# Token tiles of 1024 and 512 columns, one group's weights resident, x blocks streamed

## The chip, the cores and the metric

One of the eight cores of a Trainium2 chip runs the whole program in one launch. The metric is the device time in microseconds. An engine here is TensorE (PE), VectorE (DVE), ScalarE (ACT), GpSimd (POOL) or SyncE (SP, which issues nearly all DMAs).

## The reference, cut to what matters

A linear attention feeds two feed-forward layers. There are 8 x 576 = 4608 tokens, 512 model columns and 2048 hidden columns, all in float32.

```python
kv  = einsum('bhsd,bhse->bhde', k, v);  out = einsum('bhsd,bhde->bhse', q, kv)
x   = out / sqrt(mean(out*out, -1) + 1e-6) * g_norm        # to (4608, 512)
h   = x @ moe_w_in;   r = maximum(h, 0);  x = (r*r) @ moe_w_out       # relu layer
h   = x @ moe2_w_in;  out = (h * cos(h)) @ moe2_w_out                 # cos layer
```

The weights come in as float64 bit patterns and are turned into float32 on the chip.

## The kernel before, in words

Every float32 operand of a large product is split into a high and a low float32r part, and a product is three matmuls: high x high, high x low, low x high.

**First part.** Attention runs beside the first half of the relu layer's hidden columns, in 72 chunks (a tile of 512 tokens and one block of 128 hidden columns each). The layer's partial result goes to DRAM as `p_d`, the attention's output as `x_d`.

**Second part, in slots.** The rest of the relu layer and the whole cos layer run in a list of slots `(m, t, q)`: layer m (0 relu, 1 cos), token tile t, group q of 512 hidden columns. The relu layer has 2 groups left, the cos layer 4. Tiles are of 768 tokens, so there are 6: 12 relu slots (0 to 11) and 24 cos slots (12 to 35). The order is layer, tile, group: a tile goes through all its groups before the next tile starts.

A slot's *first product* (x times w_in) is a Winograd-Strassen scheme with 7 block products instead of 8: 7 phases of 12 matmuls in `ORDER`. It needs 7 x blocks `xb` (sums and differences of quarters of the tile, each split in two) and 7 weight tiles `wi`. `keep` (ACT), `add` (DVE) and `last` (ACT) empty the accumulators, a chain of `relu_*` or `cos_*` steps with `g_hi` (ACT) and `g_lo` (DVE) makes the operand g. The *second product* (g times w_out, 4 weight tiles `wo`) runs in units of 12 matmuls; `drain` adds each into a partial sum `part` that stays in SBUF for all groups of the tile.

Before, `prep_load` and `prep_block` make the next tile's x blocks and write them to `xb_d`; `load_xb` reads each block once per tile, and `load_wi` and `load_wo` read 11 tiles of 512 KB in every slot. `conv_w` of kind "pair" prepares the cos layer's w_in (`wi_d`) during the relu slots.

**What sets the order.** A list of jobs, each at a position in slots (`at(pos(...), fn)`), is sorted and run between matmuls; 84 first-product steps make one slot, and second-product steps of the slot before stand between them, `LAG2` later. The tile framework then places buffers and semaphores; every engine works its instructions in order, SP's DMAs too.

Of the kernel before, what the change touches and what calls it, by code (L numbers as in the profile page):

```python
# [22 lines left out]
def kernel(  # L23
# [31 lines left out]
    BIG = 768  # L55
    HT = BIG // 2
    NBIG = NT // BIG
# [20 lines left out]
    y_d = [dram.tile([P, NKC, BIG], F32, name=f"y_d{t}") for t in range(NBIG)]  # L78
    xb_d = {
        (m, t, i): dram.tile([P, 2, 2, HT], F32, name=f"xb_d{m}_{t}_{i}")  # L80
        for m in range(2)
        for t in range(NBIG)
# [73 lines left out]
    def conv_w(kind, m, f, i):  # L156
        raw = raws.pop((kind, m, f, i))
        if kind == "pair":
# [8 lines left out]
            h, l = (hl_p.tile([P, NPR, P], F32R, tag="hl", name="hl") for _ in "hl")  # L167
# [3 lines left out]
            for k, x in enumerate((h, l)):  # L171
                nc.sync.dma_start(out=wi_d[m, q][:, :, k, pp, i, :], in_=as32(x[:]))  # L172
# [170 lines left out]
    def units(b):  # L343
        return [(b, p, i) for p in range(NKC) for i in range(2)]
# [60 lines left out]
    BLOCKS = {(0, 0): 2 / 7, (1, 1): 5 / 7, (0, 1): 6 / 7, (1, 0): 1.0}  # L405
    xb, wi, wo, kept, hs, ys, parts = {}, {}, {}, {}, {}, {}, {}

    def prep_load(m, t, c, stay):
        if stay:
            raw = xb_p.tile([P, 2, BIG], F32, tag="xb", name="xraw")  # L410
        else:
            raw = pools["raw"].tile([P, 2, BIG], F32, tag="r", name="xraw")
        xraw[m, t, c] = raw
        if m == 0:
            for b, s, done, n in pieces(t * BIG, BIG, S):
                nc.sync.dma_start(out=raw[:, :, done:done + n], in_=x_d[b][:, c::2, s:s + n])
        else:
            nc.sync.dma_start(out=raw, in_=y_d[t][:, c::2, :])

    def prep_block(m, t, c, i, stay):  # L420
        raw = xraw[m, t, c]
        b11, b12, b21, b22 = (raw[:, a, s] for a in range(2) for s in (slice(0, HT), slice(HT, BIG)))
        if i in (0, 1, 4):
            src = {0: b11, 1: b21, 4: b22}[i]
        else:
            new = temp([P, HT], F32, f"xt{i}")
            x, y = {
                2: lambda: (b12, b11),
                3: lambda: (b22, xraw[m, t, c, 2][:]),
                5: lambda: (b22, b12),  # L430
                6: lambda: (b21, xraw[m, t, c, 3][:]),
            }[i]()
            nc.vector.tensor_tensor(out=new, in0=x, in1=y, op=ALU.subtract)
            xraw[m, t, c, i] = new
            src = new[:]
        if stay:
            if (m, t, i) not in xb:
                xb[m, t, i] = xb_p.tile([P, 2, 2, HT], F32R, tag="xb", name="xb")
            h, l = (xb[m, t, i][:, k, c, :] for k in range(2))
        else:  # L440
            both = temp([P, 2, HT], F32R, "xhl")
            h, l = both[:, 0, :], both[:, 1, :]
        nc.scalar.copy(out=h, in_=src)  # L443
        nc.vector.tensor_tensor(out=l, in0=src, in1=as32(h), op=ALU.subtract)
        if not stay:
            nc.sync.dma_start(out=xb_d[m, t, i][:, :, c, :], in_=as32(both[:]))

    def load_xb(m, t, i):
        xb[m, t, i] = x = xb_p.tile([P, 2, 2, HT], F32R, tag="xb", name="xb")
        nc.sync.dma_start(out=as32(x[:]), in_=xb_d[m, t, i][:])  # L450

    def load_wi(k, i):
        m, t, q = slots[k]
        wi[k, i] = w = w_p.tile([P, 2, 2, 2, P], F32R, tag="w", name="wi")
# [56 lines left out]
    def cos_1(k, b):  # L511
        ys[k, b] = y = temp([P, 2, HT], F32, "y")
        nc.scalar.activation(out=y[:].bitcast(I32), in_=hs[k, b], func=AF.Identity, bias=zerob)  # L513

    def cos_2(k, b):
        y = ys[k, b]
        nc.vector.scalar_tensor_tensor(  # L517
            out=y, in0=y[:].bitcast(I32), scalar=-1.0, in1=hs[k, b], op0=ALU.mult, op1=ALU.add
# [16 lines left out]
    def g_hi(k, b):  # L535
        gs[k, b] = g = pools["g"].tile([P, 2, 2, HT], F32R, tag="g", name="g")
        nc.scalar.copy(out=g[:, 0], in_=ys[k, b])  # L537

    def g_lo(k, b):
        g = gs[k, b]  # L540
        nc.vector.tensor_tensor(out=g[:, 1], in0=ys.pop((k, b)), in1=as32(g[:, 0]), op=ALU.subtract)  # L541

    def load_parts(t):
        for i in range(NKC):
            parts[0, t, i] = e = w_p.tile([P, BIG], F32, tag="w", name="part")
            for b, s, done, n in pieces(t * BIG, BIG, TOK):
                nc.sync.dma_start(out=e[:, done:done + n], in_=p_d[b][:, i, s:s + n])

    s_count = [0]
    units_of = (2 * NKC, BIG // P)  # L550

    def second_unit(k, n):
        m, t, q = slots[k]
        half = units_of[m] // 2
        j, i = 1 - n // half, n % half
        ps = bank_of(f"acc{s_count[0] % 4}")
        s_count[0] += 1
        if m == 0:
            ps = ps[:, :HT]
# [16 lines left out]
    def drain(k, j, i, ps):  # L576
        m, t, q = slots[k]
        final = q == groups_of[m][-1]
        if m == 0:
            e = parts[0, t, i][:, j * HT:(j + 1) * HT]  # L580
# [14 lines left out]
        if final:  # L595
            r0 = t * BIG + r * P
            nc.sync.dma_start(out=out[r0:r0 + P, :], in_=e)
# [5 lines left out]
    LAG2 = 1.2  # L603
# [8 lines left out]
    class Stream:  # L612
# [10 lines left out]
        def place(self, positions, after, skip=()):  # L623
            for k, (n, item) in enumerate(zip(positions, self.items)):
                at(n, self.use, *item)
                if k not in skip:
                    at(n + (after if n < nA0 else after / 12), self.advance)
# [26 lines left out]
    for b, (s0, ds) in enumerate(starts):  # L654
        for i, u in enumerate(units(b)):
# [17 lines left out]
    def prep(m, t, c, n0, n1, stay=False):  # L673
        at(n0 - (1.0 if stay else 0.1), prep_load, m, t, c, stay)
        for a, i in enumerate((0, 1, 2, 3, 5, 4, 6)):
            at(n0 + (n1 - n0) / NPR * a, prep_block, m, t, c, i, stay)

    for c in range(2):
        prep(0, 0, c, nAtt + 3 + 9 * c, nAtt + 11 + 9 * c, True)
    for k, (m, t, q) in enumerate(slots):  # L680
        if q:
            continue
        if k:
            for f, i in enumerate(ORDER):
                at(pos(k - 1 + f / 7 + 0.03), load_xb, m, t, i)
        following = (m, t + 1) if t + 1 < NBIG else (m + 1, 0)
        if following[0] < 2:
            n0, n1 = max(pos(k - 0.9), pos(0.2)), pos(k + len(groups_of[m]) - 1.05)
            half = (n1 - n0) / 2
            for c in range(2):  # L690
                prep(*following, c, n0 + c * half, n0 + (c + 0.9) * half)
    for k, (m, t, q) in enumerate(slots):
        early = 0.4
        for f, i in enumerate(ORDER):
            at(pos(k + f / 7 - early) if k else nA0 - 5 + f / 2, load_wi, k, i)
        for c in range(4):
            at(pos(k + LAG2 - early + 0.02 * c), load_wo, k, c)
        if m == 0 and q == 0:
            at(pos(k + LAG2 - 0.2), load_parts, t)
        at(pos(k + 1 / 7), keep, k, "m1", 0)  # L700
        at(pos(k + 2 / 7), add, k, (0, 0), 1, "m1")
        at(pos(k + 3 / 7), keep, k, "u2", 3)
        at(pos(k + 4 / 7), keep, k, "m5", 2)
        at(pos(k + 5 / 7), add, k, (1, 1), 5, "m5")
        at(pos(k + 6 / 7), add, k, (0, 1), 4, "u2")
        at(pos(k + 1.0), last, k)
        chain = (cos_1, cos_2, cos_3, cos_4, cos_5, g_hi, g_lo) if m else (relu_1, relu_2, g_hi, g_lo)
        for b, s0 in BLOCKS.items():
            for a, fn in enumerate(chain):
                at(pos(k + s0 + 0.04 * (a + 1)), fn, k, b)  # L710
# [128 lines left out]
```

## Time and profile before

| | |
|---|---|
| median of 3 runs | 1847.97 us (1846.03 to 1854.89) |
| the profiled execution | 1847.94 us, its span 1846.2 us |
| PE busy in the span | 1703.8 us, 92% |
| DVE, ACT busy | 1108.0 us (60%), 968.9 us (52%) |
| moved by DMA | 500.2 MB, mean 271 GB/s |
| granted TensorE clock, mean | 0.974 |

The span runs from the first instruction to the last. Busy shares are averages over parts with different limits, so the rows further down are cut by stretch. Matmuls overlap each other, and the records' durations of one matmul are longer than the distance between two. A line such as L475 is a line of the kernel; `FB<-xb,wi` is what an instruction writes and reads.

### The profile page before, as it was taken

To read this page: it belongs to the slowest core of one execution; us is meant where nothing else is said; L and a number is where in the kernel's file an instruction comes from. 1 tells how busy PE (TensorE), PEld (TensorE's weight loads), DVE (VectorE), ACT (ScalarE), POOL (GpSimd) and SP (SyncE) were. 2 spreads that over 40 slices of the span, in tenths; PEclk is the share of its full clock that TensorE was granted. 3 is DMA by queue.
4 is the path that set the end of the run, shared out by engine and by line. 5 is a ranking of instruction groups with operands and counts; after the bars stand their busy time and mean duration, and the time that the engine had idled before them with its cause. 6 is when DMAs were issued, how large, how long until landed. Compare 5 with 4: busy or idle time off the path is not lost.

```text
span 1846.2 us, 23727 instructions
## 1 busy us (share of the span) xinstructions
PE 1703.8 (92%) x8624; PEld 1456.2 (79%) x8624; DVE 1108.0 (60%) x1766; ACT 968.9 (52%) x1556; POOL 82.7 (4%) x74
## 2 busy tenths in 40 slices
PE   5899999999996978787878899999999999999998
PEld 3676777777785968777778798888888888888887
DVE  6866676767736555545453446666665656655554
ACT  4766677764425343433433446555565656555453
POOL 0102121221000000000000000000000000000000
PEclk9999999999998999898989999999999999999999
DMA  7655677654579999999999977987987888878551
GB/s 277 195 172 163 217 242 219 186 166 147 166 249 309 369 346 368 369 355 368 355 344 355 396 279 267 333 296 257 330 289 268 322 296 280 294 243 321 186 202 41
DMA packets 233093, 500.19 MB, mean 271 GB/s; under 512 B 19600, under 2 KB 133264, under 8 KB 232976
## 3 DMA queue, kind: packets, MB, share of 16 engines
q1 hardware_dynamic: 232208, 496.31, 77.7%
q0 software_dynamic: 768, 2.36, 0.3%
q8 instruction: 68, 1.11, 0.2%
q14 instruction: 49, 0.40, 0.1%
HBM read 365.69 MB, written 132.91 MB: 270 GB/s over the span
## 4 chain that ended last, share of the span: by engine, by line
PE 60%; DMA 10%; DVE 3%; SPq 2%; ACT 2%; issue 1%; DVEq 0%; ACTq 0%
PE SA L570 15%; PE SB L570 14%; PE FA L475 12%; PE FB L475 12%; DMA wo<-wo_d 2%; DMA wi<-wi_d 2%; PE FA L360 2%; PE SB L395 2%; PE SA L395 2%; PE FB L360 1%; DMA xraw<-x_d 1%; DMA xb_d<-xhl 1%; DMA xraw<-y_d 1%; DMA xb<-xb_d 1%; SPq L172 1%
## 5 line engine op out<-in xcount | busy, mean ns | idle before, releaser
L475 PE MATMUL FB<-xb,wi 128*128 128x384 f32 x1512 | 406.5, 347 | 40.7 <-ACT m L486 20.4
L475 PE MATMUL FA<-xb,wi 128*128 128x384 f32 x1512 | 402.9, 342 | 33.1 <-DMA wi<-wi_d 16.1
L475 PEld LDWEIGHTS FB<-xb,wi 128*128 128x128 f32 x1512 | 284.7, 194 | 54.8 <-ACT m L486 22.3
L475 PEld LDWEIGHTS FA<-xb,wi 128*128 128x128 f32 x1512 | 280.5, 191 | 45.4 <-issue 15.2
L570 PE MATMUL SB<-wo,g 128*128 128x512 f32 x864 | 309.7, 398 | 0.8 <-DVE part L590 0.8
L570 PE MATMUL SA<-wo,g 128*128 128x512 f32 x864 | 309.6, 398 | 0.8 <-DVE part L590 0.8
L570 PEld LDWEIGHTS SB<-wo,g 128*128 128x128 f32 x864 | 160.0, 187 | 37.8 <-DVE part L590 3.9
L570 PEld LDWEIGHTS SA<-wo,g 128*128 128x128 f32 x864 | 160.0, 187 | 37.5 <-DVE part L590 3.7
L513 ACT ACTIVATE y<-h,zerob 128x768 int32<-128x768 f32 x96 | 90.1, 939 | 167.0 <-DVE h L492 166.5
L570 PE MATMUL SA<-g,wo 128*128 128x384 f32 x576 | 143.8, 361 | 22.6 <-DMA wo<-wo_d 18.2
L570 PEld LDWEIGHTS SA<-g,wo 128*128 128x128 f32 x576 | 108.6, 203 | 33.7 <-DMA wo<-wo_d 24.6
L570 PE MATMUL SB<-g,wo 128*128 128x384 f32 x576 | 129.5, 343 | 5.2 <-DVE part L581 5.2
L531 DVE SCALAR_TENSOR_TENSOR y<-y,h 128x768 f32<-128x768 f32 x96 | 91.7, 955 | 63.6 <-ACT y L527 63.6
L443 ACT CAST xhl<-xraw 128x384 fp32r<-128x384 f32 x66 | 33.2, 505 | 175.6 <-DMA xraw<-x_d 120.9
L517 DVE SCALAR_TENSOR_TENSOR y<-y,h 128x768 f32<-128x768 int32 x96 | 91.7, 955 | 41.6 <-ACT y L513 40.1
L570 PEld LDWEIGHTS SB<-g,wo 128*128 128x128 f32 x576 | 105.4, 194 | 7.2 <-DVE part L581 7.0
L360 PE MATMUL FA<-xh,wh 128*128 128x512 f32 x240 | 99.3, 414 | 5.9 <-ACT xh L329 3.7
L541 DVE TENSOR_TENSOR g<-y,g 128x768 fp32r<-128x768 f32 x96 | 91.7, 956 | 21.6 <-ACT g L537 20.7
L537 ACT CAST g<-y 128x768 fp32r<-128x768 f32 x96 | 80.1, 834 | 46.5 <-DVE y L531 46.4
L523 ACT ACTIVATE y<-y 128x768 f32<-128x768 f32 x96 | 81.3, 847 | 43.1 <-DVE y L517 42.2
L360 PE MATMUL FA<-xl,wh 128*128 128x512 f32 x240 | 96.9, 404 | 0.1
L360 PE MATMUL FA<-xh,wl 128*128 128x512 f32 x240 | 96.1, 400 | 0.0
(154 smaller groups left out, 2676.4 us busy)
## 6 DMA issues: line engine op xcount, KB each, us to landing
wi<-wi_d SPq DMA_DIRECT2D x252, 512.0 KB, 5.9
wo<-wo_d SPq DMA_DIRECT2D x144, 512.0 KB, 6.5
xb_d<-xhl SPq DMA_DIRECT2D x154, 384.0 KB, 4.8
xb<-xb_d SPq DMA_DIRECT2D x77, 768.0 KB, 7.8
wi_d<-hl SPq DMA_DIRECT2D x48, 448.0 KB, 3.8
kvld<-in_kv SPq DMA_DIRECT2D x32, 512.0 KB, 6.9
raw<-in_wA SPq DMA_DIRECT2D x24, 512.0 KB, 4.1
q<-in_qT SPq DMA_DIRECT2D x32, 288.0 KB, 4.1
```

The source lines that it names most:

```text
L172: nc.sync.dma_start(out=wi_d[m, q][:, :, k, pp, i, :], in_=as32(x[:]))
L360: nc.tensor.matmul(ps, a[:, 0, cs], m[:], start=(c == 0 and k == 0), stop=(c == NKC - 1 and k == 2))
L395: nc.tensor.matmul(o, a[:, cs], m[:], start=(f == 0 and n == 0), stop=(f == NH - 1 and n == 2), skip_group_check=True)
L443: nc.scalar.copy(out=h, in_=src)
L475: nc.tensor.matmul(ps[:, pp, :], a, b, start=(i in (0, 1, 2) and n == 0), stop=(n == 5), skip_group_check=True)
L513: nc.scalar.activation(out=y[:].bitcast(I32), in_=hs[k, b], func=AF.Identity, bias=zerob)
L517: nc.vector.scalar_tensor_tensor(out=y, in0=y[:].bitcast(I32), scalar=-1.0, in1=hs[k, b], op0=ALU.mult, op1=ALU.add)
L523: nc.scalar.activation(out=y, in_=y, func=AF.Sin, scale=math.pi)
L531: nc.vector.scalar_tensor_tensor(out=y, in0=y, scalar=-2.0 * math.pi, in1=hs.pop((k, b)), op0=ALU.add, op1=ALU.mult)
L537: nc.scalar.copy(out=g[:, 0], in_=ys[k, b])
L541: nc.vector.tensor_tensor(out=g[:, 1], in0=ys.pop((k, b)), in1=as32(g[:, 0]), op=ALU.subtract)
L570: nc.tensor.matmul(ps, lhs, rhs, start=(n == 0), stop=(n == 11), skip_group_check=True)
```

## The change

- Token tiles are four of 1024 and one of 512 (`TILES`, with half size ht): matmuls of the first product have 512 or 256 columns instead of 384, and so have the relu layer's second ones.
- The list of slots is ordered layer, group, tile: 10 relu slots (0 to 9, of which 4 and 9 are the tile of 512) and 20 cos slots. A group's 11 weight tiles are loaded once, and stay for its five slots.
- In a layer's first pass (q = 0) `load_quads` reads a tile's quarters and `x_block` makes the blocks right before use, and writes them to `xb_d`; in later passes `x_block` reads both halves back, 1.9 sevenths of a slot ahead.
- Partial sums no longer stay in SBUF: `load_ev` brings each unit's sum in, `drain` adds, and the result is written to `y_d` or `o_d` (`out` in the last pass).
- A weight pair's low half is written into its raw tile, not into a tile of its own. Buffers: 13 tiles of 4 KB per partition for x, 16 for h, y and g; a pad of 96 bytes moves the tiles of the first part, and all operands of the large products then start at multiples of 128 bytes.

```diff
-    BIG = 768
-    HT = BIG // 2
-    NBIG = NT // BIG
+    BIG = 1024
+    TILES = [(t0, min(BIG, NT - t0) // 2) for t0 in range(0, NT, BIG)]
...
-            h, l = (hl_p.tile([P, NPR, P], F32R, tag="hl", name="hl") for _ in "hl")
+            p_h, tag = (pools["h"], "w") if pools["h"] is w_p else (pools["h"], "x")
+            h = p_h.tile([P, NPR, P], F32R, tag=tag, name="wh")
+            l = a.bitcast(F32R)[:, 1:]
...
-    slots = [(m, t, q) for m in range(2) for t in range(NBIG) for q in groups_of[m]]
+    slots = [(m, t, q) for m in range(2) for q in groups_of[m] for t in range(len(TILES))]
...
+    def x_block(k, i):
+        m, t, q = slots[k]
+        ht = TILES[t][1]
+        h, l = xb[k, i] = [big("x", F32R, f"x{n}", ht) for n in "hl"]
+        if q:
+            for a, x in enumerate((h, l)):
+                nc.sync.dma_start(out=as32(x), in_=xb_d[m, t, i][:, a])
+            return
...
+        if i == 3:
+            quads[m, t, "t1"] = combine(b12, b11)
+            quads[m, t, "t2"] = combine(b22, quads[m, t, "t1"])
...
         nc.scalar.copy(out=h, in_=src)
         nc.vector.tensor_tensor(out=l, in0=src, in1=as32(h), op=ALU.subtract)
+        for a, x in enumerate((h, l)):
+            nc.sync.dma_start(out=xb_d[m, t, i][:, a], in_=as32(x))
...
+    def load_ev(k, j, i):
+        m, t, q = slots[k]
+        t0, ht = TILES[t]
+        evs2[k, j, i] = e = temp([P, 512], F32, "ev")
+        if m:
+            r = j * (ht // P) + i
+            if q:
+                nc.sync.dma_start(out=e, in_=o_d[t].rearrange("p c n -> p (c n)")[:, r * DM:(r + 1) * DM])
+        elif q:
+            nc.sync.dma_start(out=e[:, :ht], in_=y_d[t][:, i, j * ht:(j + 1) * ht])
+        else:
+            for b, s0, done, n in pieces(t0 + j * ht, ht, TOK):
+                nc.sync.dma_start(out=e[:, done:done + n], in_=p_d[b][:, i, s0:s0 + n])
...
+        e = evs2.pop((k, j, i))
...
             nc.vector.tensor_tensor(out=e, in0=ps, in1=e, op=ALU.add)
-            if final and j == 0:
-                nc.sync.dma_start(out=y_d[t][:, i, :], in_=parts.pop((0, t, i)))
+            nc.sync.dma_start(out=y_d[t][:, i, j * ht:(j + 1) * ht], in_=e)
...
-    LAG2 = 1.2
+    LAG2 = 1.18
...
-        (pairs_in(1, range(2 * NP)), pos(0.4), pos(10)),
+        (pairs_in(1, range(2 * NP)), pos(2.5), pos(9.2)),
...
+    PH = 1 / 7
     for k, (m, t, q) in enumerate(slots):
+        if q == 0:
+            at(pos(k - 3.2 * PH) if k else nA0 - 6, load_quads, m, t)
         for f, i in enumerate(ORDER):
+            lead = 1.5 if q == 0 else 1.9
+            at(pos(k + (f - lead) * PH) if k or f > 2 else nA0 - 4 + f, x_block, k, i)
+            if t == 0:
+                at(pos(k + (f - 5.5) * PH) if k else nA0 - 5 + f / 2, load_wi, m, q, i)
+        if t == 0:
+            for c in range(4):
+                at(pos(k + LAG2 - 0.3 + 0.02 * c), load_wo, m, q, c)
...
+            at(pos(k + LAG2 + (n - 1.5) / len(todo)), load_ev, k, *u)
...
+        right("pad", 1).tile([P, 24], F32, name="pad")
...
+        pools["x"] = pools["h"] = ctx.enter_context(tc.tile_pool(name="xb", bufs=13, side="left"))
...
+    pools["c"] = ctx.enter_context(tc.tile_pool(name="c", bufs=16, side="left"))
+    pools["t"] = ctx.enter_context(tc.tile_pool(name="t", bufs=8, side="left"))
+    pools["h"] = w_p
```

SP's queue in the cos layer, before (L446 writes a made x block to DRAM, L450 reads one, L455 and L460 load weights):

```order
L446 DMA xb_d_2_6_159<-xhl 256x1x384
L460 DMA wo<-wo_d_11_206 128x1024
L455 DMA wi<-wi_d_3_186 128x1024 x4
L446 DMA xb_d_3_0_160<-xhl 256x1x384
L450 DMA xb<-xb_d_2_1_154 128x1536
L455 DMA wi<-wi_d_3_186 128x1024
L450 DMA xb<-xb_d_2_3_156 128x1536
```

The same queue in a later pass of the cos layer, after (L432 reads the halves of an x block, L563 a partial sum, L614 writes one):

```order
L614 DMA o_d_96<-ev 128x512
L563 DMA ev<-o_d_96 128x512
L432 DMA xh<-xb_d_2_0_150 128x1024
L432 DMA xl<-xb_d_2_0_150 128x1024
L563 DMA ev<-o_d_96 128x512
L614 DMA o_d_96<-ev 128x512
L563 DMA ev<-o_d_96 128x512
L432 DMA xh<-xb_d_2_1_151 128x1024
L432 DMA xl<-xb_d_2_1_151 128x1024
```

The weight loads are gone from between the x loads, and writes of drained units, which wait for DVE, now stand there.

DVE in the relu layer's first pass, before, while a weight pair is prepared (L433 and L444 make x blocks, L129 to L169 the pair, L541 a low part of g, L581 a drain):

```order
L129 TENSOR_SCALAR e<-raw 128x512
L131 TENSOR_SCALAR w<-raw 128x512
L444 TENSOR_TENSOR xhl<-xt_6516,xhl 128x384
L134 SCALAR_TENSOR_TENSOR w<-raw,w 128x512
L541 TENSOR_TENSOR g<-h,g 128x768
L137 SCALAR_TENSOR_TENSOR e<-raw,e 128x512
L433 TENSOR_TENSOR xt_6572<-xraw,xt_6516 128x384
L162 SCALAR_TENSOR_TENSOR raw<-w,e 128x512
L581 TENSOR_TENSOR part<-SA,part 128x384
```

The same in slot 2 after (L438 and L454 make x blocks, L129 to L171 the pair, L504 a sum, L549 a low part of g, L601 a drain):

```order
L454 TENSOR_TENSOR xl<-xraw,xh 128x1024
L549 TENSOR_TENSOR gl<-h,gh 128x1024
L601 TENSOR_TENSOR ev<-SA,ev 128x512
L601 TENSOR_TENSOR ev<-SB,ev 128x512
L129 TENSOR_SCALAR e<-raw 128x512
L131 TENSOR_SCALAR w<-raw 128x512
L134 SCALAR_TENSOR_TENSOR w<-raw,w 128x512
L137 SCALAR_TENSOR_TENSOR e<-raw,e 128x512
L601 TENSOR_TENSOR ev<-SB,ev 128x512
L162 SCALAR_TENSOR_TENSOR raw<-w,e 128x512
L504 TENSOR_TENSOR h<-FA,m_6150 128x1024
```

DVE's x work moved from halves of the next tile, long ahead, to whole blocks of the slot that is about to start, and its instructions are 1024 wide.

## Rows read from the trace of the kernel before

**Rows 1.** Busy time in four windows of the second part; columns first.
```profile
core 0: us, PE busy (x) PEld busy (x) DVE busy (x) ACT busy (x) POOL busy (x), PEclk, DMA share, GB/s
548.70:1049.10 500.40, 402.97 (x2071) 380.60 (x2070) 260.06 (x471) 204.66 (x301) 0.00 (x0) 0.92 0.99 357
1049.10:1084.60 35.50, 31.49 (x164) 30.30 (x163) 16.06 (x23) 15.83 (x21) 0.00 (x0) 0.90 0.75 288
1084.60:1787.90 703.30, 703.22 (x3439) 621.26 (x3438) 426.74 (x543) 397.81 (x521) 0.00 (x0) 1.00 0.80 281
1787.90:1846.20 58.30, 52.24 (x243) 43.81 (x241) 27.68 (x34) 22.04 (x27) 0.00 (x0) 1.00 0.25 90
```

**Rows 2.** Timeline of PE: first matmul of slots 0, 12, 13 (start, us).
```profile
548.74 0.34 PE L475 MATMUL FA<-xb,wi 128*128 128x384 f32 x1
...
1049.13 1.55 PE L475 MATMUL FA<-xb,wi 128*128 128x384 f32 x8
...
1084.57 0.33 PE L475 MATMUL FB<-xb,wi 128*128 128x384 f32 x1
```

**Rows 3.** DMA, 548.7 to 1049.1 us: total; issues, KB, us to landing.
```profile
DMA packets 99177, 178.45 MB, mean 357 GB/s; under 512 B 6351, under 2 KB 70607, under 8 KB 99148
wi<-wi_d SPq DMA_DIRECT2D x77, 512.0 KB, 8.4
xb<-xb_d SPq DMA_DIRECT2D x41, 768.0 KB, 9.5
wo<-wo_d SPq DMA_DIRECT2D x44, 512.0 KB, 9.0
```

**Rows 4.** Waits in that stretch: us in total, times, longest.
```profile
ACT xhl L443 <- DMA xraw<-x_d: 120.9, 9, 19.1
PE SA L570 <- DMA wo<-wo_d: 17.3, 10, 5.4
PE FB L475 <- DMA wi<-wi_d: 16.7, 8, 6.3
```

**Rows 5.** Chain that ended last, three places: start, us, matmuls.
```profile
482.88 2.80 PE FA L360 x12
...
1149.80 1.57 PE FB L475 x9
1151.37 1.85 PE SB L570 x8
...
1824.11 2.72 PE SB L570 x12
```

**Rows 6.** DMA between 1084.6 and 1787.9 us, as rows 3.
```profile
DMA packets 64732, 197.57 MB, mean 281 GB/s; under 512 B 6171, under 2 KB 22299, under 8 KB 64689
xb<-xb_d SPq DMA_DIRECT2D x35, 768.0 KB, 6.6
```

**Rows 7.** DVE instructions by line: busy, mean ns | idle before.
```profile
L541 DVE TENSOR_TENSOR g<-y,g 128x768 fp32r<-128x768 f32 x96 | 91.7, 956 | 21.6 <-ACT g L537 20.7
L444 DVE TENSOR_TENSOR xhl<-xt,xhl 128x384 fp32r<-128x384 f32 x88 | 48.7, 554 | 23.8 <-ACT xhl L443 22.4
L590 DVE TENSOR_TENSOR part<-SB,part 128x512 f32<-128x512 f32 x60 | 41.2, 686 | 33.3 <-PE SB L570 32.8
```

**Rows 8.** The same view: DVE work on one weight pair.
```profile
L134 DVE SCALAR_TENSOR_TENSOR w<-raw,w 128x512 uint32<-128x512 uint32 x64 | 44.0, 688 | 1.1
L131 DVE TENSOR_SCALAR w<-raw 128x512 uint32<-128x512 uint32 x64 | 26.8, 419 | 0.0
L166 DVE TENSOR_TENSOR raw<-raw 128x128 f32<-128x128 f32 x96 | 26.5, 317 | 0.6
L169 DVE TENSOR_TENSOR hl<-raw,hl 128x896 fp32r<-128x896 f32 x24 | 26.2, 1090 | 6.6 <-ACT hl L168 6.1
```

**Rows 9.** DMA issues of the whole run.
```profile
raw<-in_wA SPq DMA_DIRECT2D x24, 512.0 KB, 4.1
p_d<-ev SPq DMA_DIRECT2D x18, 512.0 KB, 4.6
```

More of the change, by code (lines that the diff above doesn't have):

```diff
@@ L77 @@
     p_d = [dram.tile([P, NKC, TOK], F32, name=f"p_d{t}") for t in range(NTILE)]
-    y_d = [dram.tile([P, NKC, BIG], F32, name=f"y_d{t}") for t in range(NBIG)]
+    y_d = [dram.tile([P, NKC, 2 * ht], F32, name=f"y_d{t0}") for t0, ht in TILES]
+    o_d = [dram.tile([P, NKC, 2 * ht], F32, name=f"o_d{t0}") for t0, ht in TILES]
     xb_d = {
-        (m, t, i): dram.tile([P, 2, 2, HT], F32, name=f"xb_d{m}_{t}_{i}")
+        (m, t, i): dram.tile([P, 2, 2, ht], F32, name=f"xb_d{m}_{t}_{i}")
         for m in range(2)
-        for t in range(NBIG)
+        for t, (t0, ht) in enumerate(TILES)
         for i in range(NPR)
@@ L420, in prep_block @@
[L420 to L432, printed above, removed]
-            nc.vector.tensor_tensor(out=new, in0=x, in1=y, op=ALU.subtract)
[L434 to L442, printed above, removed]
+    BLOCKS = {(0, 0): 2, (1, 1): 5, (0, 1): 6, (1, 0): 7}
@@ new lines, with big, load_quads @@
+    xb, wi, wo, kept, hs, ys, evs2, quads = {}, {}, {}, {}, {}, {}, {}, {}
+    def big(pool, dtype, name, ht):
+        return pools[pool].tile([P, 2, 512], dtype, tag=pool, name=name)[:, :, :ht]
+    def load_quads(m, t):
+        t0, ht = TILES[t]
+        for a in range(2):
+            for s in range(2):
+                quads[m, t, a, s] = raw = big("x", F32, "xraw", ht)
+                if m == 0:
+                    for b, s0, done, n in pieces(t0 + s * ht, ht, S):
+                        nc.sync.dma_start(
+                            out=raw[:, :, done:done + n], in_=x_d[b][:, 2 * a:2 * a + 2, s0:s0 + n]
+                        )
+                else:
+                    nc.sync.dma_start(out=raw, in_=y_d[t][:, 2 * a:2 * a + 2, s * ht:(s + 1) * ht])
@@ L535, in g_hi, with units, second_unit @@
     def g_hi(k, b):
-        gs[k, b] = g = pools["g"].tile([P, 2, 2, HT], F32R, tag="g", name="g")
-        nc.scalar.copy(out=g[:, 0], in_=ys[k, b])
+        gs[k, b] = h, l = [t_tile(k, F32R, f"g{n}") for n in "hl"]
+        nc.scalar.copy(out=h, in_=ys[k, b])
     def g_lo(k, b):
[L540 to L547, printed above, removed]
+        h, l = gs[k, b]
+        nc.vector.tensor_tensor(out=l, in0=ys.pop((k, b)), in1=as32(h), op=ALU.subtract)
+    def units(k):
+        m, t, q = slots[k]
+        half = TILES[t][1] // P if m else NKC
+        return [(j, i) for j in (1, 0) for i in range(half)]
+    def load_ev(k, j, i):
+        m, t, q = slots[k]
+        t0, ht = TILES[t]
+        evs2[k, j, i] = e = temp([P, 512], F32, "ev")
[5 more added lines that the diff above has]
+            nc.sync.dma_start(out=e[:, :ht], in_=y_d[t][:, i, j * ht:(j + 1) * ht])
+        else:
+            for b, s0, done, n in pieces(t0 + j * ht, ht, TOK):
+                nc.sync.dma_start(out=e[:, done:done + n], in_=p_d[b][:, i, s0:s0 + n])
     s_count = [0]
-    units_of = (2 * NKC, BIG // P)
-    def second_unit(k, n):
+    def second_unit(k, j, i):
         m, t, q = slots[k]
-        half = units_of[m] // 2
-        j, i = 1 - n // half, n % half
+        ht = TILES[t][1]
         ps = bank_of(f"acc{s_count[0] % 4}")
@@ L737, in run_slots @@
         seconds = [
[L738 to L740 removed]
+            (k + LAG2 + (n + a / 12) / len(units(k)), k, u, a)
+            for k in range(len(slots))
+            for n, u in enumerate(units(k))
             for a in range(12)
```

152 lines of the change are left out of this document (58 added, 94 removed).

## The prediction

> **What bounds the kernel now.** I read the busy time by stretches first, then the DMA totals and the waits of the stretch that stands out. The work has three parts. Up to 548.7 us run attention and the first half of the relu layer; then come 12 slots of the relu layer and 24 of the cos layer, a slot being one token tile of 768 with one group of weights: 84 first-product matmuls, and 96 (relu) or 72 (cos) second-product ones. Slot 0 starts at 548.74, slot 12 at 1049.13, slot 13 at 1084.57 [rows 2]. In slots 0 to 11 PE is busy 403.0 of 500.4 us at a granted clock of 0.92 (a mix of its levels 2.4 and 1.2 GHz), and the DMA engines 99% of the time at 357 GB/s [rows 1]: this stretch is bound by transfers. The waits say the same: ACT stood 120.9 us for x tiles, PE 17.3 for `wo`, 16.7 for `wi` [rows 4]. In the 22 slots from 1084.6 PE is busy 703.2 of 703.3 us at clock 1.00 (2.4 GHz), with DMA at 0.80 [rows 1]: this stretch is bound by PE, 31.97 us a slot. Whatever lies off PE matters in the first stretch, and only PE's own work in the second.
>
> **PE's work hardly changes.** In the chain, 9 matmuls of 384 columns take 1.57 us, 174.4 ns each, and 8 of 512 take 1.85, 231.3 ns; 12 on their own took 2.72 (226.7) near the end and 2.80 (233.3) before slot 0 [rows 5]. The mean durations in the page are longer because matmuls overlap; I use these distances. A line through 174.4 and 231.3 gives 118 ns for 256 columns, which no row shows. Before: first products 36 x 84 = 3024 of 384 = 527.4 us; second products 12 x 96 = 1152 of 384 = 200.9, and 24 x 72 = 1728 of 512 = 399.7; 1128.0 in all. After: 30 slots, 24 with 512 columns and 6 with 256. First: 2016 x 231.3 + 504 x 118 = 525.8. Second: 768 x 231.3 + 192 x 118 = 200.3, and 399.7. Sum 1125.8: a gain of 2 us. The bounds are what 256 columns cost: 107 ns (256 at 2.4 GHz) gives 8 us more, 174.4 (no less than 384) costs 696 x 56 = 39 us. I take 118, the line. So the change pays only by what PE waits for: 1297.5 us [rows 1] less 1128 leave 170 us of waiting.
>
> **Transfers of the relu layer, slots 0 to 9 after.** Before, 178.45 MB moved in 500.4 us [rows 3]; each slot reloads 11 weight tiles of 0.52 MB, 69 MB in 12 slots. After, weights come once per group: 22 x 0.52 = 11.5 MB. Added are the x blocks of the second pass (33.0 MB read, 33.0 written; before, 28 and 28) and the partial sums, which now go to DRAM and back between passes: 9.4 MB four times, 37.7. With 9.4 of x, 23.1 for the cos layer's weights (16 pairs read and written back) and the first tile of the cos layer it comes to 150 MB, of which about 13 stand before slot 0 in SP's order. The 137 MB left take 384 us at 357 GB/s. PE wants 364 us there: slot 0 19.4; big ones (84 + 96) x 231.3 = 41.6, six of them; slots 4 and 9 32.1; slot 5 30.8. Neither hides all of the other. Counted by where the loads stand between first products, the slots carry 6.8, 12.8, 14.5, 16.5, 8.9, 20.3, 16.3, 14.8, 14.9 and 11.9 MB; taking the larger of PE and DMA in each gives 400 us. Slot 5, where the second weights arrive and the cos layer's pairs are in full swing, is the worst: 56.9 us of transfers beside 30.8 of PE. On top I put 6 us for filling slot 0 and 6 for DVE: width costs DVE (956 - 554) / 384 = 1.05 ns an element [rows 7], 1.22 us at 1024; a big slot of the first pass has 4 differences, 7 low parts, 3 sums and 4 low parts of g, 18 x 1.22, and 8 drains at 0.69, so 27.5 us; each weight pair adds 1.09 + 4 x 0.32 + five word operations of 0.42 to 0.69, about 5.3 us [rows 8]. Six pairs now fall into slots 2.5 to 5, 32 us on top of 59, beside 94 of PE. Slots 0 to 9: 412 us against 500.4, between 384 (all overlapped) and 455 (400 stretched as slot 12 was, 35.5 us for 31.4 of PE [rows 1]).
>
> **The cos layer, slots 10 to 29.** Before, from 1049.1 to the end 797.1 us for 351.6 + 399.7 + 16.7 (slot 11's second products) = 768: 29 us lost, a third of it at the end [rows 1]. After, 761.5 (2016 and 504 become 1344 and 336 for the 20 slots: 350.5; second 399.7; slot 9's rest 11.3). I keep the 29. New are three changes of weights inside the layer; the 4.1 us that slot 12 lost is the nearest row, 12 in all. DVE in its first pass has 26 x 1.22 + 2.8 = 34.6 of 41.6 us, 83% where the third stretch has 61% [rows 1]. The free 17% and the 16 tiles that now hold h, y and g are its cover; without it PE waits for g, priced below. A pass moves 57 MB in 187.6 us, 305 GB/s; 281 GB/s [rows 6] was 80% [rows 1], so 87% busy. Sum 803, between 775 (half of the old losses) and 843 (5% lost to the two).
>
> **Before slot 0.** x tiles there move to addresses of the same residue as the rest. 12 matmuls took 2.80 us here and 2.72 where tiles already have that residue [rows 5]; if the address is the cause, 1728 x 6.7 ns = 11.5 us, if the traffic is, nothing. I take half: 543 us, 537 to 549. Splitting the x tile of slot 0 moves nearer to it and is in the 6 us above.
>
> **Sum.** 543 + 412 + 803 = 1758; the profiled run took 1.7 us beyond its span (1847.94 for 1846.2), and lies at the median of the runs, 1847.97. Forecast 1760 us, 88 less.
>
> **A rule against it.** p_d, whose rows lie 8 KB apart per partition, took 512 KB in 4.6 us, as a raw weight tile did in 4.1 [rows 9]; the new xb_d has that pitch and y_d and o_d have 16 KB, which no row shows. The Trainium skill (DMA: Bandwidth & Descriptors, Latency and other measured facts) states that row pitches at large powers of two lower the rate, 207 GB/s at 512 KiB and 103 at 4 MiB. By that rule at its worst the 94 MB of y_d and o_d would take 650 us more of DMA time; this trace shows no such loss at 8 KB, and the rule's pitches are far larger.
>
> **Rivals.**
> - *All of it hides.* Slots 0 to 9 at the 384 us of DMA, the cos layer at 775, 543 before: 1704. For it: the third stretch lost nothing at 80% DMA. Against: slot 5's bulge, and leads of 10 us.
> - *Narrow matmuls pay the full price of 384 columns*: the tile of 512 buys nothing there, 39 us more: 1799. For it: each matmul loads 128 x 128 weights whatever its width, and no row has a narrower one. Against: 384 and 512 differ by nearly what their columns take, so between them no such floor shows.
> - *x blocks arrive late and the kernel is slower.* In SP's queue every write of a drained unit stands between the x loads, and SP waits there for DVE's sum, so it can no longer run ahead; before, only final results did that. An x block of 1 MB is then issued 1.9 sevenths of a slot ahead: 1.9 x 5.94 = 11.3 us. A tile of 768 KB took 6.6 us to land in the cos layer [rows 6], 9.5 in the full stretch [rows 3]. If issue to landing takes L, each seventh lasts L / 1.9; 112 big blocks are loaded so, and the 88 us are gone at 0.79 us each, L = 12.8. At 14 us it costs 160 and the time is 1920. A second thing lengthens L: the low part of a weight pair is now made in the raw tile itself, so SP's next raw load waits until that part has landed in DRAM, and x loads queue behind it, in the relu layer only. The rows say 8 to 10 for two tiles, so mostly no; a little late (L = 12) costs 42 us: 1802.
> - *DVE falls behind in the first passes*, at 83 to 97% of PE's time; a tenth of their 360 us is 36: 1796.
>
> **Chances.** Forecast case (1735 to 1790) 0.54; all hides 0.16; one of the mild losses (narrow matmuls, DVE, loads a little late; 1790 to 1838) 0.14; these eat it all 0.05; slower by late loads 0.11, the pitch rule's share 0.02 of it. Differences of 0.5%, 9 us, are about what runs of this kernel can tell. Faster 0.84, same 0.05, slower 0.11. The likeliest case alone spans 1735 to 1790; 8 in 10 take in the rivals: 1690 to 1845.
>
> **What would show it.** Slot 0 to slot 10 in 400 to 425 us with DMA above 90% and few waits on `wi` and `wo`; 512-column matmuls 227 to 233 ns apart, 256 near 118; big cos slots of 41 to 43 us with PE never idle. I am wrong where PE waits for xh or xl block after block (late loads), where narrow matmuls stand 170 ns apart, or where the relu slots stay above 45 us at full DMA.

## The result and the profile after

The changed kernel took 1766.86 us (median of 4 runs, 1766.59 to 1768.01); the kernel before took 1848.58 beside it (4 runs, 1846.03 to 1854.89). The ratio is 0.9554, with a 95% interval of 0.953 to 0.9579: 82 us less. The profiled execution has a span of 1764.8 us. Every kernel below is cut at the same two places: A ends with the first matmul of the first product, "relu" are the slots that issue the relu layer's first products, "cos" is the rest.

| kernel | A | relu | cos | span |
|---|---|---|---|---|
| before | 548.7 | 500.4 | 797.1 | 1846.2 |
| predicted | 543 | 412 | 803 | 1758 |
| after | 544.7 | 439.1 | 781.0 | 1764.8 |

So the total was 7 us from the forecast, but two of its terms were off, by +27 and by -22 us, and cancelled.

The busy time of the changed kernel in windows, which answers to [rows 1] (columns as there). The first is slots 0 to 9, the second slots 10 to 13, the third 15 slots of the cos layer, the last the end:

```profile
core 0: us, PE busy (x) PEld busy (x) DVE busy (x) ACT busy (x) POOL busy (x), PEclk, DMA share, GB/s
544.70:983.80 439.10, 387.61 (x1700) 310.64 (x1699) 243.82 (x351) 193.12 (x213) 0.00 (x0) 0.95 0.91 314
983.80:1148.00 164.20, 157.73 (x717) 129.27 (x716) 127.79 (x126) 111.32 (x119) 0.00 (x0) 0.98 0.88 327
1148.00:1711.00 563.00, 562.64 (x2558) 460.11 (x2558) 314.52 (x333) 292.64 (x312) 0.00 (x0) 1.00 0.89 303
1711.00:1764.80 53.80, 48.42 (x246) 39.92 (x244) 25.03 (x34) 18.68 (x26) 0.00 (x0) 1.00 0.35 117
```

The relu stretch is 61 us shorter, but it is no longer full: the DMA engines are busy 0.91 of it where they were 0.99, and PE still stands idle for 51 us. In the 15 cos slots PE is busy 562.64 of 563.00 us, although all three changes of weights (at slots 15, 20 and 25) lie in them. Next, DMA in the first of these windows; [rows 3] are the rows before:

```profile
DMA packets 90764, 137.79 MB, mean 314 GB/s; under 512 B 6603, under 2 KB 58315, under 8 KB 90740
xh<-xb_d SPq DMA_DIRECT2D x28, 512.0 KB, 7.1
xl<-xb_d SPq DMA_DIRECT2D x28, 512.0 KB, 7.6
```

The bytes are as counted (137 MB predicted), and a tile lands sooner than before (7.1 to 7.6 us, where an x tile took 9.5 and a weight tile 8.4). Bytes and latency are right, then, and the rate is not. PE's waits in this window (us in total, times, longest), against [rows 4]:

```profile
PE FB L480 <- DMA xh<-xb_d: 13.6, 6, 8.9
PE SA L589 <- DVE ev L601: 7.2, 5, 3.7
PE SB L589 <- DVE ev L601: 7.1, 4, 4.2
PE FA L480 <- DMA xh<-xb_d: 6.2, 4, 1.8
PE FA L480 <- DMA xl<-xb_d: 5.2, 3, 3.3
PE FB L480 <- DMA xl<-xb_d: 3.9, 4, 2.1
```

The waits on `wi` are gone from the list, and of those on `wo` one of 2.8 us is left; PE now waits 28.9 us for x blocks that are read back, and 14.3 for DVE's partial sums. Why those are late stands in the waits of SP's own queue in the same window:

```profile
SPq L174 <- ACT wh L170: 78.4, 16, 8.4
SPq L147 <- DMA wi_d<-raw: 29.1, 13, 4.0
```

L174 is the write of a prepared weight pair to `wi_d`, L147 the load of the next raw pair. For 107.5 us SP stood at these two, with every load that came later in its queue behind it. The chain of waits shows what that does in slot 4 (start, us, what), which took 56.1 us instead of 32.1:

```profile
706.50 1.09 DVE raw L171
707.61 4.74 DMA wi_d<-raw
714.33 6.23 DMA ev<-p_d
720.68 0.70 DVE ev L601
721.42 3.03 PE SB L589 x12
```

DVE makes the low half, the half lands in DRAM, SP may reload the raw tile, only behind that does it issue the read of a partial sum, DVE adds it, and PE gets its accumulator back. SP's timeline (start, us, instruction) has the same stretch in issue order:

```profile
707.61 0.52 SPq L174 DMA_DIRECT2D wi_d<-raw  x1
...
712.36 0.90 SPq L147 DMA_DIRECT2D raw<-in_wB  x2
713.31 0.46 SPq L456 DMA_DIRECT2D xb_d<-xh  x1
713.82 0.47 SPq L456 DMA_DIRECT2D xb_d<-xl  x1
714.33 0.54 SPq L568 DMA_DIRECT2D ev<-p_d  x1
```

The raw load goes out at 712.36, when the write issued at 707.61 has landed (4.74 us in the chain); the writes of an x block and the read of the partial sum behind it follow in the next 2 us.

### The profile page after: what moved, and what is told of

It is laid out like the page before. It is cut to its first block, busy times and chain, and to the rows that moved or that the text cites. A ratio compares the mean times of both kernels' runs of the same rounds, so it can differ in the third digit from the quotient of the medians.

```text
span 1764.8 us, 22062 instructions
## 1 busy us (share of the span) xinstructions
PE 1666.6 (94%) x7928; PEld 1318.5 (75%) x7928; DVE 1085.8 (62%) x1522; ACT 943.2 (53%) x1348; POOL 82.0 (5%) x74
## 3 DMA queue, kind: packets, MB, share of 16 engines
q8 instruction: 62, 1.02, 0.2%
## 4 chain that ended last, share of the span: by engine, by line
PE 71%; DVE 9%; DMA 8%; ACT 7%; issue 3%; SPq 1%; POOL 0%; DVEq 0%; ACTq 0%; POOLq 0%
PE SA L589 14%; PE SB L589 14%; PE FA L480 12%; PE FB L480 11%; PE FA L362 8%; PE SA L397 4%; PE SB L397 4%; PE FB L362 2%; DMA xl<-xb_d 1%; DMA wi_d<-raw 1%; DMA xraw<-x_d 1%; DMA xh<-xb_d 1%; DMA ev<-p_d 1%; PE FB L241 1%; DVE h L504 1%
## 5 line engine op out<-in xcount | busy, mean ns | idle before, releaser
L480 PE MATMUL FB<-xh,wi 128*128 128x512 f32 (+1 forms) x840 | 289.7, 376 | 18.4 <-DMA xh<-xb_d 13.6
L480 PE MATMUL FA<-xh,wi 128*128 128x512 f32 (+1 forms) x840 | 285.5, 372 | 8.0 <-DMA xh<-xb_d 6.2
L589 PE MATMUL SB<-wo,gh 128*128 128x512 f32 x576 | 210.9, 397 | 1.1 <-DVE ev L606 1.1
L589 PE MATMUL SA<-wo,gh 128*128 128x512 f32 x576 | 208.6, 394 | 0.6 <-ACT gh L545 0.6
L480 PEld LDWEIGHTS FB<-xh,wi 128*128 128x128 f32 x840 | 159.6, 192 | 50.8 <-DMA xh<-xb_d 11.2
L480 PEld LDWEIGHTS FA<-xh,wi 128*128 128x128 f32 x840 | 156.9, 189 | 40.1 <-DMA xh<-xb_d 5.9
L480 PE MATMUL FB<-xl,wi 128*128 128x512 f32 (+1 forms) x420 | 158.1, 376 | 4.0 <-DMA xl<-xb_d 3.9
L480 PE MATMUL FA<-xl,wi 128*128 128x512 f32 (+1 forms) x420 | 156.2, 372 | 5.2 <-DMA xl<-xb_d 5.2
L589 PEld LDWEIGHTS SB<-wo,gh 128*128 128x128 f32 x576 | 107.5, 188 | 30.9 <-DVE ev L606 7.7
L589 PEld LDWEIGHTS SA<-wo,gh 128*128 128x128 f32 x576 | 107.5, 188 | 28.4 <-DVE ev L606 3.8
L589 PE MATMUL SA<-wo,gl 128*128 128x512 f32 x288 | 112.8, 392 | 0.2 <-DVE gl L549 0.2
L589 PE MATMUL SB<-wo,gl 128*128 128x512 f32 x288 | 112.7, 391 | 0.0
L549 DVE TENSOR_TENSOR gl<-y,gh 128x1024 fp32r<-128x1024 f32 (+1 forms) x80 | 89.1, 1114 | 33.0 <-ACT gh L545 33.0
```

Of the source, the lines that this page charges most:

```text
L480: nc.tensor.matmul(ps[:, pp, :], a, b, start=(i in (0, 1, 2) and n == 0), stop=(n == 5), skip_group_check=True)
L549: nc.vector.tensor_tensor(out=l, in0=ys.pop((k, b)), in1=as32(h), op=ALU.subtract)
L589: nc.tensor.matmul(ps, lhs, rhs, start=(n == 0), stop=(n == 11), skip_group_check=True)
```

## The experiments

All are edits of the changed kernel. The theory: tile order and resident weights made the gain, by bytes; what is left in the relu stretch is SP's queue standing at the cos layer's weight pairs; the cos layer gains by equal matmul widths. The rivals: widths made the gain; the pairs cost by their bytes and DVE work; x blocks come too late because they are issued too late.

**Order without the widths.** Slots in the new order, weights resident, x streamed, but six tiles of 768:

```diff
-    BIG = 1024
+    BIG = 768
```

> The changed kernel with six token tiles of 768 instead of four of 1024 and one of 512; the order (layer, group, tile), the resident weights and the streamed x blocks stay. Theory 1, the gain is the relu layer's transfers: the time stays near 1767, up to 18 us more, because 384 and 512 columns alternate again in the cos layer (half of it from that, half from more and shorter DVE instructions). Rival, wider matmuls and wider DVE and ACT instructions bring it: most of the 82 us is lost, 1820 to 1850.

Measured 1790.75 us (1789.62 to 1795.06), ratio 0.9692 [0.9671, 0.9712]. Its windows, relu and cos:

```profile
543.20:986.10 442.90, 388.36 (x2054) 370.73 (x2053) 250.61 (x394) 199.61 (x250) 0.00 (x0) 0.94 0.93 313
986.10:1787.80 801.70, 793.78 (x3858) 696.26 (x3857) 480.73 (x566) 439.30 (x536) 0.00 (x0) 1.00 0.86 287
```

That is 24 us above the changed kernel, where at most 18 had been expected. The order, with the resident weights and the streamed x blocks, brings the relu stretch from 500.4 to 442.9 us and does nothing for the cos layer (797.1 to 801.7). The widths bring the cos layer from there to 781.0 and nearly nothing in the relu stretch (439.1).

**The weights' bytes put back.** Eleven weight tiles are read again in every large relu slot, and never used:

```diff
+        if m == 0 and t < 4:
+            for a in range(11):
+                at(pos(k + (a + 0.5) / 11), again, m, q, a)
```

> The changed kernel with 11 tiles of 512 KB read from wi_d a second time in each of the eight big relu slots, into free weight buffers and never used: 46 MB more, none of it waited for by PE. Theory 1: the relu slots are near what the DMA engines move, so 46 MB at 314 to 357 GB/s add 100 to 147 us less what idle DMA time takes up (9% of 439 us, 40 us): 1767 + 60 to 107, 1827 to 1874. Rival, the relu layer after the change is held by SP's queue and DVE and no longer by bytes: under 25 us more.

Measured 1881.42 us (1879.58 to 1882.95), ratio 1.0177 [1.0155, 1.02]. The relu window:

```profile
546.90:1099.20 552.30, 421.67 (x1700) 328.43 (x1699) 245.12 (x349) 194.28 (x213) 0.00 (x0) 0.88 0.93 333
```

46 MB more cost 113 us in this stretch and nothing in the cos layer (780.5), a little more than expected in all (46 MB at 357 GB/s are 129 us, not the 100 of the expectation). At this window's 333 GB/s they are 138 us of transfers. A rival would be that 88 more DMAs cost SP's time: but issuing kept SP busy 224 us here and 215 in the changed kernel's stretch, and its two waits at the pairs came to 123.4 us for 107.5. So bytes are most of the price there, and taking the weights' bytes away is what paid.

**Pair writes later in SP's queue.** The two writes of a pair are queued 0.18 of a slot after the pair is made, the next raw load 0.34 after:

```diff
-            for k, x in enumerate((h[:], l)):
-                nc.sync.dma_start(out=wi_d[m, q][:, :, k, pp, i, :], in_=as32(x))
+            made[kind, m, f, i] = (h[:], l)
...
+                    at(n if n < nA0 else n + STORE, store_pair, *item)
...
-                    at(n + (after if n < nA0 else after / 8), self.advance)
+                    at(n + (after if n < nA0 else LOAD), self.advance)
```

> The changed kernel with the two writes of a finished weight pair put 0.18 slots (7 us) behind its conversion in the relu slots, and the next raw load 0.34 slots behind. Theory 2, the relu layer's 27 us beyond the forecast are SP's queue standing at these writes (78 us for ACT's copy, 29 us for the landing of the low half): both waits almost vanish and slots 0 to 9 fall from 439 to about 412: 1740. Rival a, the DMA engines are slowed by the mix of short and long runs: no change, 1760 to 1770. Rival b, DVE and ACT are behind with the pairs: no change.

Measured 1740.04 us (1739.02 to 1741.42), ratio 0.9414 [0.9396, 0.9431]. The relu window, then SP's waits for the pairs in it (the pair's write is L195 here, the raw load L148):

```profile
541.80:957.30 415.50, 377.88 (x1700) 303.47 (x1699) 242.68 (x349) 193.31 (x213) 0.00 (x0) 0.98 0.94 331
```

```profile
SPq L195 <- ACT wh L171: 45.9, 11, 8.3
...
SPq L148 <- DMA wi_d<-raw: 11.9, 8, 2.5
```

The same pairs, the same bytes and the same DVE work (242.68 us busy for 243.82): only the place in the queue differs. SP's two waits, expected almost to vanish, fall from 107.5 to 57.8 us, and the stretch by 23.6, to within 4 us of the 412 that had been predicted for it. So this is what that part of the queue's hold cost; the rest of it is still there. Part of the gain comes through TensorE's clock. In the changed kernel's stretch it was granted at 0.95, a mix of the levels 2.4 and 1.2 GHz (0.87 in slot 4, where PE stood idle for 18 of 56.1 us); here it was granted at 0.98. For the same 1700 matmuls PE was busy 377.88 us instead of 387.61: of the 23.6 us, 9.7 are faster matmuls and 13.9 less standing idle.

**Pairs spread over slots 2.5 to 22** instead of 2.5 to 9.2:

```diff
-        (pairs_in(1, range(2 * NP)), pos(2.5), pos(9.2)),
+        (pairs_in(1, range(2 * NP)), pos(2.5), pos(22)),
```

> The changed kernel with the 16 pair conversions spread over slots 2.5 to 22 instead of 2.5 to 9.2; 10 of them move to the cos layer, with 14 MB and 53 us of DVE. Theory 2: ten of 16 holds of the queue leave the relu layer, 15 to 25 us there, and cost little in the cos layer, where PE never waits from slot 14 on: 1740 to 1755. Rival a, bytes bind: 14 MB at 314 GB/s, 45 us less in the relu layer: 1722. Rival c, the holds move along and now stop the cos layer's x loads, which have no slack: 1765 to 1785.

Measured 1729.76 us, ratio 0.9354 [0.9334, 0.9375]; relu, then cos:

```profile
540.70:931.30 390.60, 370.06 (x1694) 301.46 (x1693) 200.51 (x253) 179.41 (x194) 0.00 (x0) 0.98 0.90 320
931.30:1723.50 792.20, 771.49 (x3522) 628.37 (x3520) 508.51 (x589) 436.94 (x475) 0.00 (x0) 1.00 0.88 307
```

The relu stretch falls by 48.5 us, twice as much as the later writes gave and more than the 15 to 25 that the theory gave to the holds. Ten of the 16 pairs leave it, and their bytes and DVE work (243.8 to 200.5 us) leave with the holds; what each of the three is worth was not separated. 11.2 us come back in the cos layer, where the pairs now lie.

**Both edits together.**

> The changed kernel with both: writes of a pair put behind its conversion, and the conversions spread over slots 2.5 to 22. Theory 2 (SP's queue held by the pairs, wherever they stand): the relu layer falls a little under the 390.6 us of the spread version, to 375 to 385, and the cos layer, which had risen from 781.0 to 792.2 by the pairs that moved there, comes back to 780 to 785: 1700 to 1715. Rival, what the pairs cost the cos layer is DVE and ACT time or bytes: cos stays at 790, 1720 to 1728.

Measured 1711.94 us (1707.35 to 1712.98), ratio 0.9263 [0.9239, 0.9287]. Relu 374.3, cos 792.0. The windows of the relu stretch and of slots 10 to 13:

```profile
544.80:919.10 374.30, 365.08 (x1694) 297.88 (x1693) 199.30 (x251) 178.73 (x194) 0.00 (x0) 1.00 0.93 334
919.10:1085.00 165.90, 156.99 (x714) 127.62 (x713) 143.18 (x164) 114.90 (x124) 0.00 (x0) 0.99 0.90 332
```

PE is now busy 365.08 of 374.30 us in the relu stretch, at a granted clock of 1.00: it is bound by PE. The theory had said that with the writes late the cos layer would come back to 780 to 785, and that failed: it stayed at 792. The trace says where the 11 us lie: in slots 10 and 11, and in 15, 16, 20 and 21, at two of the changes of weights (these four took 152.2 us for 144.8); slots 17 to 19 and those from 22 on take what they took. PE's waits in the cos layer are all for DVE and ACT, 15.8 us for 8.4 in the changed kernel, and none is for a DMA. So what a pair costs there is likely work on DVE (143.18 us in four slots, 127.79 without pairs) and ACT; no run separates the two.

**x blocks asked for later.**

```diff
-            lead = 1.5 if q == 0 else 1.9
+            lead = 1.5 if q == 0 else 0.9
```

> The changed kernel with the x blocks of later passes issued 0.9 sevenths of a slot ahead instead of 1.9. The prediction's rule for late loads: a seventh lasts L / lead; L is 7.0 us to landing plus 0.6 for the issue of the first half, so 7.6 / 0.9 = 8.4 us instead of 5.9; 12 big cos slots go from 41.4 to 59 us (+212), 3 small ones by 16 each, four big relu slots by 10 each: 1767 + 300, 2050 to 2080. Rival, SP runs further ahead than the positions say and the lead hardly matters: under 100 us more.

Measured 1784.03 us, ratio 0.9653 [0.963, 0.9676]: 17 us over the changed kernel, where 2050 to 2080 in all had been expected. Relu and cos, then PE's waits in the relu stretch:

```profile
547.40:998.20 450.80, 396.37 (x1700) 316.15 (x1699) 243.54 (x351) 192.51 (x213) 0.00 (x0) 0.92 0.89 308
998.20:1782.60 784.40, 768.96 (x3517) 629.02 (x3516) 467.29 (x491) 422.52 (x455) 0.00 (x0) 1.00 0.85 293
```

```profile
PE SB L589 <- DVE ev L601: 16.6, 8, 6.2
PE SA L589 <- DVE ev L601: 8.4, 5, 3.0
PE FB L480 <- DMA xh<-xb_d: 4.9, 4, 2.1
```

**x blocks asked for earlier**, the same line with 3.2 instead of 1.9:

> The changed kernel with the x blocks of later passes placed 3.2 sevenths of a slot ahead instead of 1.9. In its trace SP issued them 26.9 us ahead of use in the cos layer and 7.9 us in the relu layer, where a half lands in 7.1 to 7.6 us. Theory 4: only the relu layer's second pass can gain; PE waited there 29 us for xh and xl, and half to all of that goes: 1738 to 1755. Rival, these loads are late because SP's queue stands at the weight pairs, and a place further ahead in the same queue does not help: 1760 to 1770.

Measured 1758.15 us, ratio 0.951 [0.9484, 0.9537], between what the theory gave and what the rival gave; relu 429.7, cos 783.7. Between the issue of an x block on SP and its first matmul there lie, by the median of the large tiles:

| lead in the code | relu, second pass | cos, passes 2 to 4 |
|---|---|---|
| 1.9 sevenths (11.3 us) | 7.9 us, least 5.9 | 26.9 us, least 16.3 |
| 0.9 | 8.7 | 26.6 |
| 3.2 | 10.2 | 29.0 |

A lead of 0.9 sevenths, 5 us, did not make the cos layer late: the loads still went out 27 us ahead. So the position in the list of jobs is not what sets the issue; what does, no run here shows. Nor are the 27 us fixed: in the two versions with the pairs spread, at 1.9, the median in the cos layer is 12.7 us, and PE hardly waits for an x block there either (0.7 us). My expectation of a loss in the cos layer rested on the list alone, and fell. In the relu stretch the real lead is 8 to 10 us (medians) for tiles that land in 7 to 8. There the stretch is 11.7 us longer at 0.9 and 9.4 shorter at 3.2, but not by late x blocks alone: PE's waits for them come to 28.9 us at 1.9, 13.5 at 0.9 and 22.0 at 3.2, and those for DVE's sums to 14.3, 25.0 and 17.5. At 0.9 the time rose while the x waits fell, so the rival is not borne out, and what the setting changes there stays open. The next kernel, which is unchanged in this stretch, took 444.4 us for 439.1, so that part of both differences may be scatter.

**No pad of 96 bytes** at the start of the buffers of the first part:

```diff
-        right("pad", 1).tile([P, 24], F32, name="pad")
```

> The changed kernel without the 96 bytes of pad: the tiles of the first part are back at 32 bytes beyond a multiple of 64. Prediction's half: the distance between matmuls there grows by up to 6.7 ns and the time by 6 us. After the result I expect less: runs of 12 take 2.79 us with the pad and took 2.80 without, 1 ns a matmul, so 0 to 2 us. Rival, the address is what brought the first part's 4 us: 4 to 5 us more.

Measured 1770.63 us, ratio 0.958 [0.9555, 0.9605], an interval that overlaps that of the changed kernel. The chain of waits of the one with the pad, then of the one without, in the first part:

```profile
484.61 2.79 PE FA L362 x12
```

```profile
481.98 2.80 PE FA L362 x12
```

Twelve matmuls take 2.79 us with the pad and 2.80 without, as before [rows 5]. The address is not the cause of 2.80 beside 2.72. Part A varies from 540.7 to 547.4 us between kernels that don't differ there, so that its 4 us less than before can't be told from nothing.

**Tiles of 768 with matmuls in runs.** As the first experiment, but second products are given out only every 12 first ones, so that 384 and 512 columns alternate less often:

```diff
-            while ns < len(seconds) and seconds[ns][0] <= here:
+            while n % 12 == 0 and ns < len(seconds) and seconds[ns][0] <= here:
```

> The version with six tiles of 768, with second products given out in whole runs at every 12th first-product step, so that runs of 384 and of 512 columns follow each other and single ones no longer alternate. Theory 3, the cos layer's 20.7 us (781.0 against 801.7) are the price of alternating widths (176 + 236 ns a pair against 174 + 227 in runs): cos slots fall from 32.2 to about 31.1 us, 24 x 1.1 = 26 us, to 1765 or a little over. Rival, they come from the number of instructions or of slots (fixed cost of each matmul, of each phase): no change, 1790.

Measured 1781.09 us, ratio 0.9646 [0.962, 0.9672]: 9.7 less than in alternation, cos 788.3 us for 801.7, a cos slot 31.6 for 32.2. The chain of waits with alternation (FA is a first-product matmul of 384, SB a second-product one of 512), then in runs:

```profile
1303.71 0.24 PE SB L589
1303.95 0.18 PE FA L480
1304.13 0.24 PE SB L589
```

```profile
1304.75 2.10 PE FB L480 x12
1306.85 2.54 PE SA L589 x11
```

A pair of 512 and 384 takes 0.41 to 0.42 us alternating and 0.175 + 0.231 = 0.406 in runs. In the changed kernel a 512 stands beside a 512, and 11 or 12 of them in a row take no more than alternating ones, 0.226 each:

```profile
1224.38 2.49 PE FA L480 x11
1226.87 0.23 PE FB L480
1227.10 2.72 PE SA L589 x12
1229.82 0.23 PE SB L589
```

Of the 20.7 us that the widths gave the cos layer, runs alone give 13.4, where 26 had been expected. Another 6.5 are in the prediction's count of PE's work, 768.0 us with tiles of 768 and 761.5 with the new ones; 5.4 of these only because the last relu slot leaves 11.3 us of second products to the cos layer instead of 16.7. Under 1 us stays open.

**The two SP edits and runs where widths still differ.** In and right behind the slots of the tile of 512 a 256 stands beside a 512; there second products are given out every 6 first ones:

```diff
+            k0 = min(n // 84, len(slots) - 1)
+            mixed = slots[k0][1] == 4 or k0 and slots[k0 - 1][1] == 4
-            while ns < len(seconds) and seconds[ns][0] <= here:
+            while (not mixed or n % 6 == 0) and ns < len(seconds) and seconds[ns][0] <= here:
```

> The version with both edits to the pairs, and in the 11 slots where the tile of 512 meets one of 1024 second products given out only at every sixth first-product step, so that widths alternate less. Theory 3 (alternating widths cost 5 to 10 ns a pair): a mixed slot falls by 0.5 to 1.0 us as the slots of 768 did (32.2 to 31.6): 5 to 10 us less than 1711.9, 1702 to 1707. Rival, nothing: 1712.

Measured 1706.11 us (1705.02 to 1707.21), ratio 0.9234 [0.9214, 0.9254]: the fastest, 61 us below the changed kernel. It is 5.8 us below the two edits alone, as expected, but the intervals of the two ratios overlap, and the slots do not bear the reason out: the 11 where widths mix take 391.9 us together for 395.0, and the undisturbed ones among them, 14, 19 and 24, take 32.4 us in both versions, where each was to fall by 0.5 to 1.0. That runs help beside 256 columns is not shown.

## Why the prediction was right, and where it was not

**What bounds the kernel, and the bytes: right.** The relu stretch was bound by transfers; 46 MB put back cost 113 us, and the changed kernel moves the 137.8 MB that were counted as 137. Most of the gain lies there, 61 of 82 us, where 88 had been predicted. That the total came within 7 us is luck: +27 and -22 us cancelled.

**Slots 0 to 9: the mechanism right, the size wrong.** 412 was the sum, 439 the time. I took the larger of PE and DMA in each slot, 400, with slot 5 the worst because of its bytes, and gave the rest 12 us. (The upper bound beside it is a slip: 400 stretched by 35.5 / 31.4 is 452, not 455.) The slots that stood out were 4 (56.1 us for 32.1 of PE), 5 (51.3 for 56.9 predicted) and 8 (51.6 for 41.6). What the term lacked is that the DMA engines run out of work while SP stands at a pair's write: 0.91 busy at 314 GB/s where I took 357. At 357 the bytes would take 386. Idle engines are not all of it: 314 at 0.91 is 345 GB/s while busy, 357 at 0.99 was 361, and no run tells why. Of the hold I had named one part as the second thing that lengthens L, the raw load that waits until the low half has landed (29.1 us), and gave it no price in the forecast. The larger part, the write that waits for ACT's copy (78.4 us, and 22.0 in the stretch before the change), I had not named. Moving both in the queue took off half of these waits and 23.6 us. Nor had the sum a term for the clock; it counts every matmul as at 2.4 GHz. The clock was granted at 0.95, and PE was busy 387.61 us for the 364 counted; at 1.00, with both edits, it was busy 365.08. By the prediction's own signs this stretch went partly wrong: not 400 to 425 us, and slots 3 to 8 took 45.7 to 56.1, above the 45 that had been named, though with DMA at 0.91 and not full.

**The cos layer: 803 predicted, 781.0 measured.** The priced work of PE, 761.5, was right to within what can be told: five slots of the steady stretch take 187.6 us (a third of 563.0), four times that and 11.3 for slot 9's rest make 761.7. What failed is the losses on top, 41 us, measured 19. The 29 lost that I carried over were largely no waits: before, a cos slot of 31.97 us is 84 x 174.4 + 72 x 231.3 ns, 31.3 us, and 0.67 more, 16 us in 24 slots. The experiment in runs, with tiles of 768 in the new order, shows 0.6 of it to be alternation of widths, which the changed kernel has only in and behind the slots of 512. And the 12 for three changes of weights were nothing: all three lie in the 563 us with PE busy throughout. What is left is 10 at the end, as before, and 9 in slots 10 to 13 (164.2 us; the like slots 15 to 18 take 155.0).

**Narrow matmuls: right.** 256 columns had been put at 118 ns from the line through 384 and 512. Eleven of them in the chain of waits of the changed kernel:

```profile
1158.07 1.32 PE FA L480 x11
```

120 ns each. The rival that they cost as much as 384 columns is dead.

**Late x blocks: the rival was rightly improbable, for a wrong reason.** Its lead of 11.3 us came from the list of jobs; the real one is 27 us in the cos layer, and no x block was late there. In the relu stretch it is 8, and PE waited 28.9 us for x blocks; 11.7 with the pairs' writes later and the same lead in the code, so most of that was SP standing at the pairs and not the lead.

**DVE behind in the first passes: priced at 36 us for two passes, and at most 9 came in the cos layer's** (slots 10 to 13, with DVE busy 127.79 of 164.20 us). In the relu layer's it can't be told from SP's holds, which also make DVE's sums late.

**The pad: I took half of 11.5 us, and nothing can be shown.** The stretch A came out near 543 by its scatter.

**The pitch rule: no loss of its size.** DMA issues of the third window (KB each, us to landing):

```profile
ev<-o_d SPq DMA_DIRECT2D x101, 256.0 KB, 5.1
o_d<-ev SPq DMA_DIRECT2D x86, 256.0 KB, 4.8
...
xh<-xb_d SPq DMA_DIRECT2D x21, 256.0 KB, 4.3
```

Partial sums, with 16 KB from partition to partition (8 in the tile of 512), take 4.8 to 5.1 us, and the same bytes of a small x block, with 4 KB, 4.3; PE waits for neither here. The row pitches for which the Trainium skill (DMA: Bandwidth & Descriptors, Latency and other measured facts) gives a loss begin at 512 KiB, which no run here has.

## What to carry to other kernels

When a change takes bytes out of a stretch bound by transfers, price what is left by the rate at which the issuing queue can keep the engines fed, not by the rate that the old, full stretch reached: look in the queue's own waits for writes that wait for a compute engine, and put them later in the queue than the loads they would hold up. Before carrying an old loss over to a new kernel, find out what it is made of: an excess that comes with every slot while PE is busy throughout belongs to PE's work and goes with the shapes. A total that comes out right shows nothing about its terms; compare them stretch by stretch.

## What was not expected of the hardware

Matmuls of two widths that alternate take a little longer than the two widths in runs: 512 and 384 columns 0.41 to 0.42 us a pair against 0.406, and a cos slot of 768 tokens 32.2 us against 31.6. Equal widths show no difference (226 to 227 ns either way). What in PE causes it no run here tells.

SP's DMAs for the cos layer's x blocks went out 27 to 29 us before use (medians) whether the code asked for 0.9, 1.9 or 3.2 sevenths of a slot, 5, 11 or 19 us, and 12.7 us before use, at 1.9, once weight pairs were made in the cos layer too. What gives this lead was not looked into.
